# Reordering a start-up stretch: an MLP unit ahead of attention's states, two weight pieces moved forward, one filler product less

## The chip, the cores and the metric

The kernel runs on one core of a Trainium2 chip. The metric is the device time of one execution in microseconds (us). A run here means: the kernel is profiled once, its output is compared with the reference, and it is timed in several rounds that alternate with the kernel before on the same chip. Every execution reports its span and the mean clock that was granted to TensorE (1.000 is full speed). All ratios below are computed as the mean time of one kernel's fast executions over the mean time of the other's in the same rounds, with a 95% interval, so they are not quite the ratio of the medians that are quoted beside them.

Line numbers (L426 and so on) are lines of the kernel that was profiled. The change inserts lines, so one statement has two numbers; these are used below:

| statement | before | after |
|---|---|---|
| first-layer products of a unit, `plain_unit` | L426 | L435 |
| second-layer products, `plain_out` | L405 | L409 |
| activation's last step on VectorE, `plain_relu` | L442 | L453 |
| filler products "idle" | L842 | L853 |
| transposes of a part's k and q | L695 | L706 |
| scores, states | L714, L734 | L725, L745 |
| values: own chunk, then earlier chunks | L762, L773 | L773, L784 |
| running sums of the states on VectorE | L746 | L757 |
| transposes of the third part's k and q | L789 | L800 |
| weight piece: three steps on VectorE, one on GpSimd | L307, L310, L312; L314 | L310, L313, L315; L318 |
| scaling of q, k, v on GpSimd | L675 | L686 |

## The reference

Attention without a softmax, with a decay per head, and then an MLP with a PReLU, all in float32 (the constants are filled in here):

```python
# q, k, v: (8, 8, 576, 64)
scores = 64 ** -0.5 * q @ k.T                  # per batch and head
ret    = scores * where(i >= j, gamma[h] ** (i - j), 0)
attn   = ret @ v
x      = attn, heads side by side              # (4608, 512)
h      = x @ w_in                              # w_in (512, 2048)
g      = maximum(h, 0) + alpha * minimum(h, 0)
out    = g @ w_out                             # w_out (2048, 512)
```

## The kernel before

Nearly all of the time is TensorE's MLP. The change touches only the start: the first sequence's attention is computed in three "parts" (256, 256 and 64 positions), the weights are brought in as "pieces" that ScalarE, VectorE and GpSimd convert, and the first MLP "units" are put between them as soon as their inputs exist. The program issues instructions in the order of these calls, and in the traces an instruction stands behind the one ahead of it on its engine (the prediction below shows a wait of 1.99 us on VectorE that held up the piece behind it):

```python
    piece_out(2)
    part_carry(0)
    part_values(0)
    for _ in range(2):                     # filler: keeps TensorE at work
        nc.tensor.matmul(idle, ident, ...)
    nc.tensor.transpose(aps, a16, ...)
    ...
    plain_unit(0, 0)                       # the first unit
    plain_relu()
    piece_out(1)                           # the fifth piece
    part_scale(1, 2)                       # scaling of v, second part
    part_transposes(1, 0)
    piece_in(1)
    mlp_out(lambda: part_transposes(1, 1))
    piece_out(1)                           # the sixth piece
    piece_in(1)
    part_scores(1)
    piece_out(1)                           # the seventh piece
    part_states(1)                         # TensorE products, then four sums on VectorE
    piece_in(1)
    plain_unit(0, 1)                       # the second unit
    piece_out(1)                           # the eighth piece
    part_scale(2, 1)                       # scaling of q, third part
    plain_relu()
    piece_in(1)
    part_values(1)
    part_scale(2, 2)
    part_carry(1)
    last_transposes()                      # the third part's k and q
    mlp_out()                              # output products of the second unit
```

`piece_in` issues ScalarE's step of a weight piece, `piece_out` the three steps on VectorE and the one on GpSimd. `plain_unit` issues 8 products (16 records in the trace) and ScalarE's two activations; `plain_relu` issues VectorE's step after them.

Of the kernel before, what the change touches and what calls it, by code (L numbers as in the profile page):

```python
# [10 lines left out]
FP32 = mybir.dt.float32  # L11
INT32 = mybir.dt.int32
UINT32 = mybir.dt.uint32
ACTF = mybir.ActivationFunctionType
ALU = mybir.AluOpType
# [3 lines left out]
def kernel(  # L19
# [10 lines left out]
    nc = tc.nc  # L30
# [3 lines left out]
    P = 128  # L34
# [6 lines left out]
    NCC = DM // P  # L41
    NFC = DFF // P
    NU = NFC // 2
    HM = DM // 2
# [24 lines left out]
    def half(x):  # L69
        return slice(x * C, (x + 1) * C)  # L70
# [70 lines left out]
    def room(i, s0, n):  # L141
        return w_out[i][:, s0:s0 + n].rearrange("p s f -> p (s f)")
# [50 lines left out]
    for i in range(NBIT - 1):  # L193
        nc.vector.scalar_tensor_tensor(out=dif[:, i + 1], in0=dif[:, i], scalar=2.0,
                                       in1=dif[:, i], op0=ALU.add, op1=ALU.mult)
# [6 lines left out]
                            op=ALU.mult)  # L202
    nc.vector.tensor_scalar(pf, pf, 1.0, None, ALU.add)

    for o, x, y in ((slice(0, 2), slice(0, 2), slice(3, 5)), (0, 0, 1), (0, 0, 2), (1, 0, 5)):
# [7 lines left out]
                                   in1=pf[:, 6], op0=ALU.mult, op1=ALU.mult)  # L213
# [17 lines left out]
    for h2 in range(2):  # L231
# [6 lines left out]
                                       in1=tabx[hd, :, 0], op0=ALU.add, op1=ALU.mult)  # L238
# [13 lines left out]
    HI_MAX = float(np.array([0x47EFFFFF], np.uint32).view(np.float32)[0])  # L252
    HI_MIN = float(np.array([0x38000000], np.uint32).view(np.float32)[0])
# [31 lines left out]
    def piece_in(n):  # L285
        for _ in range(n):
            if npiece[1] == len(pieces):
                return
            at = npiece[1]
            npiece[1] += 1  # L290
            fetch(at + 1)
            raw, t = raws.pop(0)
            raw = raw.rearrange("p (x f two) -> p x f two", x=2, two=2)
            lo, hi = raw[:, :, :, 0], raw[:, :, :, 1]
            a = wraw.tile([P, 2, HM], FP32, tag="wa", name=f"wa_{at}")
            nc.scalar.activation(a, hi.bitcast(FP32), ACTF.Abs)

            nc.scalar.activation(lo, lo.bitcast(UINT32), ACTF.Copy, scale=2.0 ** -29)
            half_done.append((at, a, lo, hi, t))

    def piece_out(n):
        for _ in range(min(n, len(half_done))):
            at, a, lo, hi, t = half_done.pop(0)
            dst = pieces[at][1]

            c = ps_h.tile([P, 2, HM], INT32, tag="psh1", name=f"wc_{at}")
            nc.vector.tensor_scalar(c.bitcast(FP32), a, HI_MIN, HI_MAX, ALU.max, ALU.min)  # L307


            nc.vector.tensor_scalar(c, c, 3, 0x3FFFFFF8,  # L310
                                    ALU.logical_shift_left, ALU.bitwise_and)
            nc.vector.scalar_tensor_tensor(out=dst.bitcast(INT32), in0=hi, scalar=-0x40000000,  # L312
                                           in1=c, op0=ALU.bitwise_and, op1=ALU.bitwise_or)  # L313
            nc.gpsimd.tensor_tensor(out=dst.bitcast(INT32), in0=dst.bitcast(INT32), in1=lo,  # L314
                                    op=ALU.add)  # L315
            free.append(t)
            fetch(at + 1 + AHEAD)

# [100 lines left out]
    def plain_unit(kb, i):  # L419

        ph = (ps_a.tile([P, 2, TB], FP32, tag="psa", name=f"ph_{kb}_{i}") if (kb, i) == (1, 1)
              else ps_h.tile([P, 2, TB], FP32, tag="psh0", name=f"ph_{kb}_{i}"))
        g = mlp.tile([P, 8, P], FP32, tag="g", name=f"g_{kb}_{i}")
        for cc in range(NCC):
            for x in range(2):
                nc.tensor.matmul(ph[:, x], w_in[i // UST][:, cc // 2 * 2 + x, i % UST, cc % 2],  # L426
                                 xb[kb][:, cc], start=(cc == 0 and x == 0),
                                 stop=(cc == NCC - 1), skip_group_check=True)

        nc.scalar.activation(g[:, 4:8].rearrange("p x t -> p (x t)"),  # L430
                             ph.rearrange("p x t -> p (x t)"), ACTF.Relu, scale=-1.0)
        nc.scalar.activation(ph.rearrange("p x t -> p (x t)"),
                             ph.rearrange("p x t -> p (x t)"), ACTF.Relu)
        relus.append((kb, i, g, ph))

    relus = []
# [1 line left out]
    def plain_relu():  # L438
        kb, i, g, ph = relus.pop(0)
        for x in range(2):  # L440
            fc = x * NU + i
            nc.vector.scalar_tensor_tensor(  # L442
                out=g[:, 2 * x:2 * x + 2].rearrange("p m t -> p (m t)"),
                in0=g[:, 4 + 2 * x:6 + 2 * x].rearrange("p m t -> p (m t)"),
                scalar=nalpha[:, fc:fc + 1], in1=ph[:, x], op0=ALU.mult, op1=ALU.add)
        pend.append((kb, i, g))
# [98 lines left out]
    def chunk(j):  # L545
        return slice(j * C, (j + 1) * C)
# [122 lines left out]
    def part_scale(x, i):  # L669

        j0, j1 = PARTS[x]
        t = part[x][i]
        for m in range((j1 - j0 + 1) // 2):
            rows = min(P, (j1 - j0) * C)
            nc.gpsimd.tensor_tensor(  # L675
                out=t[0:rows, m], in0=t[0:rows, m],
                in1=tp[0:rows, i - 1, m, :, None].to_broadcast([rows, H, D]), op=ALU.mult)
# [26 lines left out]
    def part_scores(x):  # L704
        at = tat[x] = (mlp.tile([P, 8 * P], FP32, tag="g", name=f"pa_{x}") if x == 0 else
                       room(4, 0, 4)).rearrange("p (h n) -> p h n", h=2)  # L706
        banks = part_banks(x, 2 if x == 0 else None, "ps")
        kT, qT = tT[x, 0], tT[x, 1]
        for m in range(2):
            for c in range(NPAIR):  # L710
                for p2 in range(2):
                    for h2 in range(2):
                        j = chunk(2 * m + p2)
                        nc.tensor.matmul(banks[h2][half(p2), (2 * c + m) * C:(2 * c + m + 1) * C],  # L714
                                         kT[half(h2), c, j], qT[half(h2), c, j],
                                         start=True, stop=True)
        for h2 in range(2):
            to, fro = [t.rearrange("p (n s) -> p n s", s=C) for t in (at[:, h2], banks[h2])]
            m = mask[:, None, :].to_broadcast([P, 8, C])
            if x == 0:  # L720
                nc.vector.tensor_tensor(out=to, in0=fro, in1=m, op=ALU.mult)
            else:
                nc.scalar.copy(to, fro)
                nc.gpsimd.tensor_tensor(out=to, in0=to, in1=m, op=ALU.mult)

    def part_states(x):
        kn, vn = part[x][0], part[x][2]
        banks = [t.rearrange("p (m c d) -> p m c d", m=2, c=NPAIR)
                 for t in part_banks(x, None if x == 0 else 0, "pu")]
        for m in range(2):  # L730
            for c in range(NPAIR):
                for p2 in range(2):
                    for h2 in range(2):
                        nc.tensor.matmul(banks[p2][half(h2), m, c], kn[half(p2), m, 2 * c + h2],  # L734
                                         vn[half(p2), m, 2 * c + h2],
                                         start=(m == 0 and c == 0),
                                         stop=(m == 1 and c == NPAIR - 1), skip_group_check=True)
        was = carry[x]
        for j in range(4):
            u = banks[j % 2][:, j // 2]  # L740
            if x == 0:
                nc.scalar.copy(sums[x][j], u)
                if j:
                    nc.gpsimd.tensor_tensor(out=sums[x][j], in0=was, in1=sums[x][j], op=ALU.add)
            else:  # L745
                nc.vector.tensor_tensor(out=sums[x][j], in0=was, in1=u, op=ALU.add)  # L746
            was = sums[x][j]
# [90 lines left out]
    part_values(0)  # L838

    idle = ps_h.tile([P, DM], FP32, tag="psh0", name="idle")  # L840
    for _ in range(2):
        nc.tensor.matmul(idle, ident, part[0][0][:, 0].rearrange("p h d -> p (h d)"),  # L842
                         start=True, stop=True)
    aps = ps_a.tile([P, NFC], FP32, tag="psa", name="aps")
# [5 lines left out]
    piece_out(1)  # L850
    part_scale(1, 1)
    plain_unit(0, 0)
    plain_relu()  # L853
    piece_out(1)
    part_scale(1, 2)
    part_transposes(1, 0)
    piece_in(1)
    mlp_out(lambda: part_transposes(1, 1))
    piece_out(1)
    piece_in(1)  # L860
    part_scores(1)
    piece_out(1)
    part_states(1)
    piece_in(1)
    plain_unit(0, 1)
    piece_out(1)
    part_scale(2, 1)
    plain_relu()
    piece_in(1)
    part_values(1)  # L870
    part_scale(2, 2)
# [6 lines left out]
    piece_in(2)  # L878
    piece_out(2)
    plain_unit(1, 0)  # L880
    plain_relu()
    piece_in(1)
# [99 lines left out]
    n = 2 * NPAIR  # L982
    for b in range(2, B):
# [3 lines left out]
        at = [u + (u % NU == 0) for u in (c * nq // NPAIR + 2 for c in range(NPAIR))]  # L987
        if b == 2:
            at = [0, 3] + at[1:]
# [42 lines left out]
```

## Time and profile before

| | kernel before |
|---|---|
| time | 1011.77 us median of 3 (1010.21 to 1013.02); with three executions more, beside the changed kernel, 1011.2 |
| span of the profiled execution | 1008.5 us |
| TensorE busy | 99% |
| mean granted clock, profiled execution | 0.999 |

First the page of the kernel before: the granted clock and the share of the DMA engines in 40 slices of the span (in tenths), and the DMA queues (packets, MB, share of 16 engines).

```profile
PEclk9999999999999999999999999999999999999999
DMA  9986744232322222031122222323222000000000
...
q8 instruction: 74, 1.21, 0.5%
```

In the first 50 us, two slices, the DMA engines are busy 90% or more (a share of 0.97 from 0 to 50 us). Queue q8 carries instructions, in 74 packets of 16 KB. The kernel has 9389 TensorE products and as many weight loads; 18,778 / 74 is 254 instructions a packet. By this count, an estimate, q8 is TensorE's own queue, and a packet holds some 127 product records with their weight loads. (The page has a second queue of instructions, q14, with 33 packets and 0.27 MB: too few to be TensorE's by the same count.)

Then TensorE's timeline of the kernel before. The columns of a timeline are start, length, engine, line, operation and shape, the number of records, and in brackets the idle time before it and what ended it.

```profile
14.71 0.42 PE L773 MATMUL pv<-pT,w_out 64*32 64x64 f32 x14
16.35 1.21 PE L773 MATMUL pv<-pT,w_out 64*32 64x64 f32 x82 [1.22 <-issue]
...
36.34 1.16 PE L762 MATMUL pv<-w_out,w_out 64*64 64x64 f32 x64
37.43 1.91 PE L773 MATMUL pv<-w_out,w_out 64*32 64x64 f32 x128
```

### The profile page before, as it was taken

Reading aid. Unit: us, or ns where it says so; the run is one execution under the profiler, and the core shown is the slowest. Engines: PE = TensorE matmul, PEld = TensorE weight load, DVE = VectorE, ACT = ScalarE, POOL = GpSimd, SP = SyncE. Lnnn points to the kernel's source line nnn. Section 1 sums busy time; section 2 is a strip of 40 time slices with the busy share of each in tenths; the row PEclk is TensorE's granted clock in tenths of the full one; section 3 lists DMA queues with packets and bytes.
Section 4 is the critical chain, followed back from the end, with each engine's and each line's share of the span. In section 5 each row is a group of like instructions: output and inputs, shape, how many; then the busy total and the mean of one; then the engine's idle time right before and its main releaser. Section 6 shows DMA issues by size and latency. Waiting matters only on the chain.

```text
span 1008.5 us, 23133 instructions
## 1 busy us (share of the span) xinstructions
PE 995.2 (99%) x9389; PEld 891.9 (88%) x9389; DVE 773.4 (77%) x2086; ACT 267.3 (27%) x605; POOL 179.0 (18%) x201
## 2 busy tenths in 40 slices
PE   6999999999999999999999999999999999999998
PEld 5666668999999999999999999999999999999997
DVE  7769968887878778687777788878788776666665
ACT  5656652322222222022022121222222210000000
POOL 5656674210200020100020000200010001010000
PEclk9999999999999999999999999999999999999999
DMA  9986744232322222031122222323222000000000
GB/s 236 252 194 150 182 74 109 49 72 48 69 48 65 53 42 63 13 69 31 40 48 51 40 52 44 70 48 69 48 43 52 13 22 1 22 1 22 1 22 22
DMA packets 229595, 64.30 MB, mean 64 GB/s; under 512 B 214368, under 2 KB 223088, under 8 KB 229488
## 3 DMA queue, kind: packets, MB, share of 16 engines
q1 hardware_dynamic: 227088, 62.02, 27.4%
q8 instruction: 74, 1.21, 0.5%
q10 hardware_dynamic: 2400, 0.79, 0.4%
q14 instruction: 33, 0.27, 0.1%
HBM read 53.35 MB, written 9.44 MB: 62 GB/s over the span
## 4 chain that ended last, share of the span: by engine, by line
PE 98%; DMA 1%; issue 0%; DVE 0%; ACT 0%; SPq 0%; DVEq 0%
PE ph L470 40%; PE po L388 38%; PE ph L426 6%; PE po L405 6%; PE pv L652 3%; PE ps L616 1%; PE ps L622 1%; DMA w_out<-in_k_dram 1%; PE pv L966 1%; PE pt L695 0%; PE ps L714 0%; PE pv L773 0%; PE ps L559 0%; PE pu L734 0%; PE pu L577 0%
## 5 line engine op out<-in xcount | busy, mean ns | idle before, releaser
L388 PE MATMUL po<-w_out,g 128*128 128x256 f32 x1792 | 408.1, 379 | 0.0
L388 PEld LDWEIGHTS po<-w_out,g 128*128 128x128 f32 x1792 | 330.7, 190 | 39.7
L481 DVE TENSOR_TENSOR g<-ph,g 128x256 f32<-128x256 f32 (+1 forms) x512 | 187.0, 386 | 134.0 <-PE ph L470 67.7
L470 PE MATMUL ph<-xb,w_in 128*128 128x128 f32 x2048 | 272.7, 276 | 0.0
L470 PEld LDWEIGHTS ph<-xb,w_in 128*128 128x128 f32 x2048 | 257.1, 192 | 7.4 <-issue 0.5
L470 PE MATMUL ph<-xt,w_in 128*128 128x128 f32 x1536 | 213.3, 275 | 0.0
L470 PEld LDWEIGHTS ph<-xt,w_in 128*128 128x128 f32 x1536 | 192.1, 192 | 0.0
L476 ACT COPY g<-ph 128x128 f32<-128x128 f32 x128 | 34.1, 266 | 404.4 <-PE ph L470 391.9
L492 DVE TENSOR_TENSOR g<-g 128x128 f32<-128x128 f32 x512 | 129.4, 293 | 7.0
L531 POOL TENSOR_TENSOR qx<-qx,tabx 128x576 f32<-128x576 f32 x28 | 32.7, 1168 | 353.2 <-DMA qx<-in_q_dram 180.1
L486 DVE SCALAR_TENSOR_TENSOR g<-g 128x512 f32<-128x512 f32 x128 | 89.8, 701 | 3.0
L484 DVE TENSOR_SCALAR g<-g,alpha 128x256 f32<-128x256 f32 x256 | 85.8, 377 | 3.7
L405 PE MATMUL po<-w_out,g 128*128 128x512 f32 x128 | 58.6, 599 | 0.8 <-DVE g L442 0.8
L426 PE MATMUL ph<-xb,w_in 128*128 128x256 f32 x256 | 58.6, 383 | 0.0
L663 ACT COPY xb<-pv 128x256 f32<-128x256 f32 (+3 forms) x84 | 23.2, 315 | 126.5 <-PE pv L652 126.5
L426 PEld LDWEIGHTS ph<-xb,w_in 128*128 128x128 f32 x256 | 47.9, 190 | 9.3 <-issue 2.4
L600 ACT COPY vn<-su 64x512 f32<-64x512 f32 x56 | 34.5, 616 | 78.3 <-DVE su L594 77.9
L636 DVE SCALAR_TENSOR_TENSOR mt<-ps,th,mask 64x256 f32<-64x256 f32 x96 | 46.4, 483 | 2.2
L456 POOL TENSOR_TENSOR xt<-xb 128x256 f32<-128x256 f32 x16 | 11.6, 727 | 196.9 <-PE ph L470 196.9
L405 PEld LDWEIGHTS po<-w_out,g 128*128 128x128 f32 x128 | 23.4, 190 | 24.4 <-issue 22.8
L629 DVE SCALAR_TENSOR_TENSOR mt<-pv,th,mask 64x64 f32<-64x64 f32 x48 | 13.6, 283 | 40.2 <-ACT xb L663 39.8
L536 ACT ACTIVATE vn<-vn,tabv 64x576 f32<-64x576 f32 x56 | 43.2, 772 | 1.8 <-DMA vn<-in_v_dram 0.5
(136 smaller groups left out, 737.9 us busy)
## 6 DMA issues: line engine op xcount, KB each, us to landing
out_dram<-osb SPq DMA_DIRECT2D x34, 256.0 KB, 2.1
kx<-in_k_dram SPq DMA_DIRECT2D x112, 72.0 KB, 2.5
qx<-in_q_dram SPq DMA_DIRECT2D x112, 72.0 KB, 2.9
vn<-in_v_dram SPq DMA_DIRECT2D x56, 144.0 KB, 3.3
kn<-in_k_dram SPq DMA_DIRECT2D x56, 144.0 KB, 3.8
raw<-in_moe_w_in_dram SPq DMA_DIRECT2D x24, 256.0 KB, 4.4
raw<-in_moe_w_out_dram SPq DMA_DIRECT2D x10, 512.0 KB, 4.5
w_in<-in_moe_w_out_dram SPq DMA_DIRECT2D x6, 512.0 KB, 5.6
```

The costliest lines, as they stand in the source:

```text
L388: nc.tensor.matmul(acc[kb][n // 2][:, n % 2, :], g[:, x, :], w_out[i][:, y, :], start=(i == 0 and n % 2 == 0), stop=(i == NU - 1 and (n % ...
L405: nc.tensor.matmul(acc[kb][m], g[:, 2 * x + m], w_out[i][:, 2 * x:2 * x + 2].rearrange("p x f -> p (x f)"), start=(i == 0 and x == 0), sto ...
L426: nc.tensor.matmul(ph[:, x], w_in[i // UST][:, cc // 2 * 2 + x, i % UST, cc % 2], xb[kb][:, cc], start=(cc == 0 and x == 0), stop=(cc == N ...
L470: nc.tensor.matmul(ph[m][:, o], w_in[i // UST][:, l, i % UST, cc], r[:, cc], start=(n in (0, 3) and cc == 0), stop=(n in (2, 6) and cc == ...
L476: nc.scalar.copy(g[:, 7], ph[0][:, 2])
L481: nc.vector.tensor_tensor(out=o, in0=x0, in1=x1, op=ALU.add)
L484: nc.vector.tensor_scalar(g[:, 4 + 2 * m:6 + 2 * m], g[:, 2 * m:2 * m + 2], 0.0, alpha[:, fc:fc + 1], ALU.min, ALU.mult)
L486: nc.vector.scalar_tensor_tensor(out=g[:, 0:4].rearrange("p x t -> p (x t)"), in0=g[:, 0:4].rearrange("p x t -> p (x t)"), scalar=0.0, in1 ...
L492: ins = nc.vector.tensor_tensor(out=g[:, o, :], in0=g[:, x0, :], in1=g[:, x1, :], op=op)
L536: nc.scalar.activation(vn[x, h2], vn[x, h2], ACTF.Copy, scale=tabv[x, c:c + 1])
L600: nc.scalar.copy(vn[half(h2), h2, 1:], su[half(h2)])
L636: nc.vector.scalar_tensor_tensor(out=mt[to, h2, p2:NJ - 1:2], in0=ps[p2][half(x), 0], scalar=th[to, 3, h:h + 1], in1=mask[to, None, :].to_ ...
```

## The change

Its intent: let the second unit start without waiting, ahead of the second part's states, and bring the pieces that it needs forward on VectorE and GpSimd; start the first unit earlier, by one filler product less and by doing the piece and the activations that it needs in halves (the last products of that unit are put in an order that completes one half sooner). The diff, cut to its core:

```diff
-            nc.vector.tensor_scalar(c.bitcast(FP32), a, HI_MIN, HI_MAX, ...)
-            ... (two more on VectorE, one on GpSimd, 512 elements)
+            for f in (slice(0, P), slice(P, HM)) if at == 1 else (slice(0, HM),):
+                ... (the same four, for the second piece in two halves of 256)
@@ plain_unit
+        ... (for the first unit: the last four products sorted by half)
-        nc.scalar.activation(g[:, 4:8], ph, ACTF.Relu, scale=-1.0)
-        nc.scalar.activation(ph, ph, ACTF.Relu)
+        for x in (slice(0, 1), slice(1, 2)) if alone else (slice(0, 2),):
+            ... (the same two; for the first unit in two halves)
@@ the order of the start
-    for _ in range(2):
+    for _ in range(1):
         nc.tensor.matmul(idle, ...)
...
     plain_unit(0, 0)
+    piece_out(1)
     plain_relu()
-    piece_out(1)
-    part_scale(1, 2)
     part_transposes(1, 0)
     piece_in(1)
     mlp_out(lambda: part_transposes(1, 1))
     piece_out(1)
+    part_scale(1, 2)
     piece_in(1)
     part_scores(1)
+    plain_unit(0, 1)
     piece_out(1)
+    plain_relu()
     part_states(1)
     piece_in(1)
-    plain_unit(0, 1)
     piece_out(1)
     part_scale(2, 1)
-    plain_relu()
     piece_in(1)
     part_values(1)
```

## The prediction

> **What bounds the kernel now.** I read the page first, then busy time by stretches, then the timelines of TensorE (PE), VectorE (DVE) and GpSimd (POOL) up to 60 us, and last the order of instructions per engine of both kernels.

> ```profile
> PE 995.2 (99%) x9389; PEld 891.9 (88%) x9389; DVE 773.4 (77%) x2086; ACT 267.3 (27%) x605; POOL 179.0 (18%) x201
> ```

> TensorE is busy 99% of the span of 1008.5 us. The stretches say where its idle time ends:

> ```profile
> 20.00:30.00 10.00, 9.19 (x68) 6.18 (x70) 7.31 (x14) 6.88 (x14) 7.17 (x7) 1.00 0.98 255
> 30.00:40.00 10.00, 8.90 (x330) 7.66 (x321) 8.03 (x15) 6.10 (x12) 9.47 (x9) 1.00 1.11 298
> 40.00:50.00 10.00, 10.00 (x56) 7.03 (x54) 5.67 (x11) 5.80 (x13) 2.76 (x3) 1.00 0.80 179
> ```

> The third column is PE busy. From 40 us on there is no gap left, so whatever the change does has to happen before about 44 us, and TensorE's delay or lead there passes unchanged to the end. The change touches exactly this stretch. Idle time between 20 and 40 us is 0.81 + 1.10 = 1.9 us, and two dummy products ("idle") hide up to another 2. No version of this change can reach 2% (20 us).

> TensorE, in order of time (start, length, line, operation):

> ```profile
> 17.49 1.98 PE L842 MATMUL idle<-w_out,ident 128*128 128x512 f32 x4
> 19.62 3.69 PE L426 MATMUL ph<-xb,w_in 128*128 128x256 f32 x16
> 25.09 1.95 PE L405 MATMUL po<-w_out,g 128*128 128x512 f32 x4 [0.81 <-DVE g L442]
> 29.57 1.16 PE L714 MATMUL ps<-w_out,w_out 64*64 64x64 f32 x64
> 30.55 1.11 PE L734 MATMUL pu<-w_out,w_out 64*64 64x64 f32 x62
> 32.49 0.27 PE L734 MATMUL pu<-w_out,w_out 64*64 64x64 f32 x2 [0.83 <-issue]
> 32.69 3.72 PE L426 MATMUL ph<-xb,w_in 128*128 128x256 f32 x16
> 39.61 0.71 PE L789 MATMUL pt<-ident,w_out 64*128 64x64 f32 x8 [0.27 <-ACT xb L779]
> 40.24 3.70 PE L405 MATMUL po<-w_out,g 128*128 128x512 f32 x8
> ```

> L426 is a unit of the MLP (the first at 19.62, the second at 32.69), L405 its output products, L714/L734 the scores and states of attention's second part, L789 the transposes of its third part. The 0.83 us at 32.49 is put down to "issue", but the next instruction, the second unit, needs the sixth weight piece, which GpSimd finishes at 30.77 + 1.30 = 32.07; I read the gap as that wait. It is what the change wants to remove.

> VectorE, then GpSimd, in the same form:

> ```profile
> 24.47 0.87 DVE L442 SCALAR_TENSOR_TENSOR g<-g,nalpha,ph 128x256 f32<-128x256 f32 x2 [1.99 <-ACT ph L432]
> ...
> 32.11 0.41 DVE L746 TENSOR_TENSOR w_out<-w_out,pu 128x256 f32<-128x256 f32 x1
> 32.80 1.33 DVE L746 TENSOR_TENSOR w_out<-w_out,pu 128x256 f32<-128x256 f32 x3 [0.28 <-PE pu L734]
> 34.05 0.69 DVE L307 TENSOR_SCALAR wc<-wa 128x512 f32<-128x512 f32 x1
> ...
> 37.57 0.87 DVE L442 SCALAR_TENSOR_TENSOR g<-g,nalpha,ph 128x256 f32<-128x256 f32 x2 [1.38 <-ACT ph L432]
> ```

> ```profile
> 30.77 1.30 POOL L314 TENSOR_TENSOR w_in<-w_in,raw 128x512 int32<-128x512 int32 x1
> ...
> 36.32 1.30 POOL L314 TENSOR_TENSOR w_out<-w_out,w_in 128x512 int32<-128x512 int32 x1 [0.53 <-issue]
> 37.57 2.04 POOL L675 TENSOR_TENSOR w_out<-w_out,tp 64x512 f32<-64x512 f32 x2
> ```

> L442 is the activation's last step, L746 the four running sums of the states. L307 at 34.05 begins the eighth weight piece on VectorE; GpSimd adds its low bits at 36.32 and then scales q and v of the third part (L675). The second half of the L789 transposes reads that q. So a chain runs: sums, eighth piece on VectorE, eighth piece on GpSimd, scaling of q (done 37.57 + 1.02 = 38.6), transposes at 39.61. It has about 1 us of slack.

> [...] VectorE sits idle 1.99 us ahead of L442 at 24.47 while the fifth piece, next in its order, starts only at 25.26. This decides the case: who stands behind an instruction that waits, waits with it. [...] The trace has 0.69 us for 512 elements and 0.42 us for the L746 form of 256, so two halves cost more than one whole. [...] this trace grants 1.00 throughout the stretch [...].

> **The change part by part**, times in the trace's clock:

> 1. One dummy product of two goes: 1.98 / 2 = 0.99 us. The first unit also needs its first inputs: the last copy of the first half of xb ends about 18.33 and the first piece about 16.81 + 1.27 = 18.08. So it starts near 18.75 instead of 19.62 and ends near 22.2.
> 2. The second piece by halves: six instructions of about 0.40 us pitch for three of 0.72: 2.4 against 2.2 us, and about 0.3 with dispatch. VectorE is 0.3 us later from 18.3 on; the fourth piece ends at 22.48 + 0.3 = 22.8.
> 3. The first unit's activations by halves: ScalarE can finish all four near 23.1 instead of 24.43. Of little use because of the next point.
> 4. The fifth piece now stands ahead of L442 on VectorE and takes 2.15 us (24.47 less 22.48 was idle, 2.0 us): 22.8 to 24.95. L442 starts at 24.95 instead of 24.47, and the first output products, 0.62 us after, at 25.55 instead of 25.09: **0.5 us later** in spite of the earlier unit. The lead of point 1 is lost in this wait, and k of the second part lands only about 22.6 and 23.4 (issues at 17.23 and 17.95 plus the median of 5.4 us), so the transposes ahead gain little either.
> 5. Everything up to the scores keeps that delay: scores from 30.05 to 31.05. The sixth piece is done on VectorE at 25.75 + 2.15 = 27.9, on GpSimd, now ahead of the scaling of v, at about 29.3. So the second unit has no wait: 31.05 to 34.6, 1.6 us ahead of before (32.69). The states follow, 34.6 to 35.6. To this point TensorE has gained: before, unit and states were both done at 36.3.
> 6. But on VectorE the second unit's L442 now stands ahead of the four sums, and the sums ahead of the eighth piece. The steps after the unit's start are those of before: 3.76 us to ScalarE's first activation (32.69 to 36.45), 1.12 to L442: 31.05 + 4.88 = 35.95. L442 takes 0.8, the sums 4 x 0.42 = 1.67: the eighth piece starts on VectorE at 38.4, **4.3 us later** than 34.05. VectorE is idle from about 32.2 to 35.95.
> 7. From there, with the pitches of before: VectorE done 38.4 + 2.15 = 40.55; GpSimd 40.65 to 41.95; q scaled at 42.95; some 0.3 us for the wait, 0.3 us for four transposes, and the second unit's output products start at 43.6 instead of 40.24. TensorE meanwhile ends the values near 38.8 and stands for about 4 us.

> Sum: 43.6 - 40.24 = **+3.4 us**. The step before it (values) gained 0.5, the new wait costs 3.9. From here TensorE has no gap in which to win anything back. I round to 3.2, as the first transposes (k) may absorb a little: 1011.77 + 3.2 = 1015.0.

> **The rivals.**
> A. The intended gain. TensorE loses the 0.83 us wait and most of the dummy's 0.99, and nothing new waits: about 1 to 1.8 us faster, 1010.0 to 1010.8. For it: the wait is real, and up to the states my own working has TensorE ahead. Against it: the order of VectorE and of GpSimd is fixed in the program, and the eighth piece has to pass both ahead of q's scaling. It would be true if that scaling were not needed by L789, but the order view shows a wait on GpSimd at its second half.
> B. A wash. The transposes or other stages wait for DMA anyway (DMA share 0.98 to 1.11 between 20 and 40 us), and gains and losses are both hidden: 1011 to 1013. Against it: pieces and parts up to the eighth land by the time they are needed, since the waits in this stretch are on engines.
> C. [...], 1017 to 1018.5. [...]

> **Range and chances.** I give my working some 75%, A and B together 18%, C 7%. Times of before spread by 1.4 us each way. That gives 1015.0, a range from 1010.8 to 1018.0. Faster or slower by 2% would take 20 us out of a stretch of 25, hence 0.5% and 1%.

> **What would show it.** Right: a TensorE gap of 3 to 4 us ending near 43 us, ahead of the second half of the third part's transposes, released by GpSimd's scaling; the eighth piece on VectorE near 38.4, just after the sums; VectorE idle over 3 us ahead of the second unit's L442; the second unit at about 31 us without a wait; the first output products at 25.5. Wrong: output products of the second unit at or before 40.2 us, or the eighth piece on VectorE ahead of 36 us. Then the order that I followed is not what held TensorE, and A or B is true. A granted clock below 1.00 between 40 and 50 us would mean C.

## More of the kernel before

In the first part's values there is a pause of 1.22 us in the middle of a tile, after 14 of 96 products, put down to "issue": nothing that the profile shows was waited for. And the second part's values run through, x64 and x128, without a pause.

## The result and the profile after

The changed kernel took 1016.84 us (median of 6, 1016.36 to 1018.0) beside 1011.2 us of the kernel before (6 executions, 1010.21 to 1013.02): ratio 1.0056, interval 1.0043 to 1.0068. It is 0.6% slower, clearly so and within the 2% called the same. All values of the changed kernel are above all of the kernel before.

From the page of the changed kernel, the busy time and the clock:

```profile
PE 997.9 (98%) x9387; PEld 893.0 (88%) x9387; DVE 771.8 (76%) x2089; ACT 267.3 (26%) x607; POOL 180.0 (18%) x202
...
PEclk9899999999999999999999999999999999999999
```

One slice of PEclk fell from 9 to 8. That digit was the first sign of something that the prediction gave 7%. Busy time by stretches of the changed kernel (length, then busy time and records of PE, PEld, DVE, ACT and POOL, then granted clock, DMA share, GB/s):

```profile
20.00:30.00 10.00, 8.53 (x40) 5.97 (x39) 8.98 (x15) 6.93 (x16) 5.84 (x5) 0.93 1.03 260
30.00:40.00 10.00, 9.36 (x261) 7.17 (x260) 4.25 (x10) 6.39 (x12) 7.04 (x6) 1.00 1.11 287
40.00:50.00 10.00, 7.67 (x95) 4.65 (x95) 4.38 (x7) 5.05 (x10) 5.10 (x5) 0.66 0.81 178
```

Between 40 and 50 us TensorE was busy 10.00 us before and is busy 7.67 us now, and what it did there ran at a mean clock of 0.66. TensorE's timeline of the changed kernel:

```profile
14.48 0.42 PE L784 MATMUL pv<-pT,w_out 64*32 64x64 f32 x14
17.28 1.63 PE L784 MATMUL pv<-pT,w_out 64*32 64x64 f32 x82 [2.38 <-issue]
18.84 2.07 PE L853 MATMUL idle<-w_out,ident 128*128 128x512 f32 x2
...
21.06 3.82 PE L435 MATMUL ph<-xb,w_in 128*128 128x256 f32 x16
...
27.23 1.96 PE L409 MATMUL po<-w_out,g 128*128 128x512 f32 x4 [1.47 <-DVE g L453]
...
31.70 1.16 PE L725 MATMUL ps<-w_out,w_out 64*64 64x64 f32 x64
32.80 3.72 PE L435 MATMUL ph<-xb,w_in 128*128 128x256 f32 x16
36.45 1.16 PE L745 MATMUL pu<-w_out,w_out 64*64 64x64 f32 x64
37.43 1.11 PE L773 MATMUL pv<-w_out,w_out 64*64 64x64 f32 x64
38.47 0.89 PE L784 MATMUL pv<-w_out,w_out 64*32 64x64 f32 x48
41.76 1.81 PE L784 MATMUL pv<-w_out,w_out 64*32 64x64 f32 x80 [2.40 <-issue]
43.60 0.69 PE L800 MATMUL pt<-ident,w_out 64*128 64x64 f32 x4
44.83 0.69 PE L800 MATMUL pt<-ident,w_out 64*128 64x64 f32 x4 [0.54 <-POOL w_out L686]
45.45 5.25 PE L409 MATMUL po<-w_out,g 128*128 128x512 f32 x8
50.63 0.68 PE L809 MATMUL ps<-w_out 64*64 64x64 f32 x16
```

Three things are new. The second part's values have a pause of 2.40 us after x48, in the middle of a tile and without a releaser. The wait for GpSimd's scaling of q, which the prediction put at about 4 us, shows only 0.54. And the eight output products at 45.45 take 5.25 us where they took 3.70: the clock records have TensorE at half rate (a granted clock of 0.50) from 17.89 to 21.30 and from 41.78 to 48.61 us.

VectorE and GpSimd of the changed kernel, in the same form:

```profile
37.67 0.87 DVE L453 SCALAR_TENSOR_TENSOR g<-g,nalpha,ph 128x256 f32<-128x256 f32 x2 [4.13 <-PE pu L745]
38.46 1.85 DVE L757 TENSOR_TENSOR w_out<-w_out,pu 128x256 f32<-128x256 f32 x4
40.23 0.69 DVE L310 TENSOR_SCALAR wc<-wa 128x512 f32<-128x512 f32 x1
```

```profile
42.50 1.28 POOL L318 TENSOR_TENSOR w_out<-w_out,w_in 128x512 int32<-128x512 int32 x1 [5.12 <-issue]
43.74 2.04 POOL L686 TENSOR_TENSOR w_out<-w_out,tp 64x512 f32<-64x512 f32 x2
```

This chain is the predicted one: VectorE idle 4.13 us, activation, sums, eighth piece at 40.23, q scaled at 43.74 + 1.02 = 44.76.

Where the time went, step by step through the two profiled executions (start times on TensorE; the spans differ by 1015.2 - 1008.5 = 6.7 us):

| stretch of TensorE (first row: start of the scores; others: length, start to start) | before | after | difference |
|---|---|---|---|
| start to the second part's scores | 29.57 | 31.70 | +2.13 |
| scores to the values (unit and states between) | 6.77 | 5.73 | -1.04 |
| values to the third part's transposes | 3.27 | 6.17 | +2.90 |
| transposes to the second unit's output products | 0.63 | 1.85 | +1.22 |
| the eight output products | 3.64 | 5.18 | +1.54 |
| sum | | | +6.75 |

The sum of the rows is the whole difference of the spans: nothing is won or lost after 51 us. The intended gain is in the second row. The loss that belongs to the change is in the three rows below it. The first row is mostly the first pause (2.38 us against 1.22) and the half rate after it, with 0.7 us of step 4 below; an experiment below shows that the kernel before has it at that length too, so about 1 us of the 6.7 is chance between two profiled executions, and the timed 5.6 us is the figure to go by.

### The profile page after: what moved, and what is told of

Same layout as the page of the kernel before. It is cut to its first block, busy times and chain, and to the rows that moved or that the text cites.

```text
span 1015.2 us, 23135 instructions
## 1 busy us (share of the span) xinstructions
PE 997.9 (98%) x9387; PEld 893.0 (88%) x9387; DVE 771.8 (76%) x2089; ACT 267.3 (26%) x607; POOL 180.0 (18%) x202
## 4 chain that ended last, share of the span: by engine, by line
PE 97%; DVE 1%; DMA 1%; issue 0%; POOL 0%; ACTq 0%; DVEq 0%; POOLq 0%
PE ph L481 40%; PE po L392 38%; PE po L409 6%; PE ph L435 5%; PE pv L663 3%; PE ps L627 1%; PE ps L633 1%; DMA w_out<-in_q_dram 1%; PE pv L977 1%; PE ps L570 0%; DVE wc L313 0%; PE ps L725 0%; DVE wc L310 0%; PE pu L588 0%; PE idle L853 0%
## 5 line engine op out<-in xcount | busy, mean ns | idle before, releaser
L611 ACT COPY vn<-su 64x512 f32<-64x512 f32 x56 | 34.5, 617 | 78.6 <-DVE su L605 78.3
```

The lines of the kernel that those rows point to most:

```text
L611: nc.scalar.copy(vn[half(h2), h2, 1:], su[half(h2)])
```

## The experiments

All twelve runs gave correct results. The theory at the start was that of the prediction: the wait for the scaling of q costs the time. The rivals were the other parts of the change, and, after the first four runs, the pause marked "issue" and the clock.

### The other parts alone: undo_second_unit

The changed kernel, with the second unit back behind the states:

```diff
-    plain_unit(0, 1)
     piece_out(1)
-    plain_relu()
     part_states(1)
     piece_in(1)
+    plain_unit(0, 1)
     piece_out(1)
     part_scale(2, 1)
+    plain_relu()
```

> The changed kernel with the second unit put back behind the second part's states, all else changed. Theory O (order on VectorE: the second unit's activation and the four sums stand ahead of the eighth piece, so GpSimd scales the third part's q late and its transposes wait): nearly all of the 5.6 us goes, 1011.3 to 1012.5 us, eighth piece on VectorE back to about 34.5 us, no TensorE wait on the scaling of q. Rival F (the fifth piece ahead of the first unit's activation, the halves and the dropped dummy cost it): stays above 1014.5 us.

Measured: 1011.49 us beside 1011.7 us, ratio 0.9996 (0.9981 to 1.0011). One filler product less, the halves, and the fifth and sixth piece forward are together a wash. TensorE's timeline of this run is odd all the same:

```profile
26.46 1.96 PE L409 MATMUL po<-w_out,g 128*128 128x512 f32 x4 [1.85 <-DVE g L453]
...
40.14 1.16 PE L784 MATMUL pv<-w_out,w_out 64*32 64x64 f32 x80 [1.66 <-issue]
```

The wait on the activation is longer than the 0.81 us of the kernel before, and the pause after x48 of the values is here too, although the second unit is where it was. The granted clock was 1.00 up to 60 us (0.999 over the whole profiled execution), and the four executions had 0.998 to 1.000.

### The second unit alone: only_second_unit

The kernel before with the reverse of that edit:

```diff
+    plain_unit(0, 1)
     piece_out(1)
+    plain_relu()
     part_states(1)
     piece_in(1)
-    plain_unit(0, 1)
     piece_out(1)
     part_scale(2, 1)
-    plain_relu()
```

> The kernel before with only the second unit moved ahead of the states (its activation with it); two dummies, whole first unit, old places of the fifth and sixth piece. Theory O: most of the loss is there, 1014.5 to 1016.5 us, with the eighth piece on VectorE at about 40 us and the wait on the scaling of q. Rival F: 1011 to 1012.5 us.

Measured: 1016.78 us, ratio 1.0054 (1.0035 to 1.0072), with clocks of 0.995 and 0.996. The move of the second unit makes the whole loss. Its timeline has the pause after x47, 3.02 us long, and then half rate. No wait for the scaling of q shows in it: the transposes run as one block of eight.

```profile
41.03 1.88 PE L773 MATMUL pv<-w_out,w_out 64*32 64x64 f32 x81 [3.02 <-issue]
42.93 1.27 PE L789 MATMUL pt<-ident,w_out 64*128 64x64 f32 x8
44.12 5.15 PE L405 MATMUL po<-w_out,g 128*128 128x512 f32 x8
```

### The wait for q taken away: scale_first

```diff
     part_states(1)
+    part_scale(2, 1)
     piece_in(1)
     piece_out(1)
-    part_scale(2, 1)
     piece_in(1)
```

GpSimd scales q before the eighth piece, at 36.73 us in the trace, so nothing waits for it.

> The changed kernel with the scaling of the third part's q put ahead of the eighth piece on GpSimd; VectorE's order untouched. Theory O alone: the transposes no longer wait, the output products of the second unit start 1.2 us earlier than 45.45 if the 2.4 us gap in the values (put down to issue) and the half clock stay: about 1015.5 us. Rival I (the gap put down to issue and the half clock after it are a consequence of the order too and go with it): 1011 to 1013 us.

Measured: 1015.03 us, ratio 1.0032 (1.0013 to 1.0051). Some two of nearly six microseconds come back; more than three stay. TensorE's timeline of this run:

```profile
40.51 1.16 PE L784 MATMUL pv<-w_out,w_out 64*32 64x64 f32 x80 [1.82 <-issue]
41.94 1.00 PE L800 MATMUL pt<-ident,w_out 64*128 64x64 f32 x8 [0.28 <-ACT xb L790]
42.87 5.02 PE L409 MATMUL po<-w_out,g 128*128 128x512 f32 x8
```

The transposes run as one block of eight, so the predicted wait is gone, and the kernel is still slow. So the wait is not the only cause, and it is not needed for a loss of 3 us.

### The eighth piece early: eighth_early and eighth_early_b

Both put the eighth piece ahead of the second unit's activation on VectorE.

```diff
@@ eighth_early
     piece_out(1)
-    plain_relu()
-    part_states(1)
     piece_in(1)
     piece_out(1)
+    plain_relu()
+    part_states(1)
     part_scale(2, 1)
```

> The changed kernel with the eighth piece moved on ScalarE, VectorE and GpSimd ahead of the second unit's activation, into VectorE's idle 4.1 us. Theory O: the wait on q's scaling goes; eighth piece on VectorE at 33.6 us, q scaled before 40.5 us. With the 2.4 us issue gap and the half clock staying: about 1015.5 us; if these go too: 1010 to 1012 us.

Measured: 1016.01 us, ratio 1.0038 (1.0015 to 1.006). This edit was a mistake of mine: `plain_unit` issues ScalarE's activations itself, so the eighth piece's step on ScalarE stayed behind the unit, the piece reached VectorE only at 38.06, and the sums went back to 40.91. It is still of use for one thing: its four executions had different clocks, 1013.18 us at 1.000, 1014.82 at 0.998, 1017.62 at 0.995 and 1017.19 at 0.994. One kernel on one chip spread over 4 us, in the order of its clock but for the last pair.

The second attempt moves ScalarE's step as well:

```diff
@@ eighth_early_b
     part_scores(1)
+    piece_in(1)
     plain_unit(0, 1)
-    piece_out(1)
+    piece_out(2)
     plain_relu()
     part_states(1)
-    piece_in(1)
-    piece_out(1)
     part_scale(2, 1)
```

> As eighth_early, but with ScalarE's step of the eighth piece ahead of the second unit too, which was missed there (its activations are issued with the unit). Theory O: the eighth piece is on VectorE by 35 us, q scaled by 40 us, TensorE does not wait for it. Then only the gap put down to issue in the values is left of the new waits: 1.1 to 1.9 us better than the changed kernel, 1014.5 to 1015.8 us. If that gap was caused by the late sums or pieces, it is gone too: below 1013 us.

Measured: 1015.87 us beside 1012.09 us, ratio 1.0038 (1.0016 to 1.0061). The eighth piece is on VectorE at 35.54 us and q is scaled at 40.5 us; the wait on GpSimd is gone. What is left is the pause and the clock:

```profile
43.08 1.16 PE L784 MATMUL pv<-w_out,w_out 64*32 64x64 f32 x80 [2.82 <-issue]
...
45.55 6.41 PE L409 MATMUL po<-w_out,g 128*128 128x512 f32 x8
```

### The kernel before once more: before_again

No edit; one look, to see which pauses the kernel before has from run to run.

> The kernel before, once more, for its profile. If the first gap put down to issue (1.22 us in the values of the first part, in front of the dummies) belongs to the kernel, it is again near 1.2 us; if it varies by run, it may be 2.0 to 2.4 us as in all changed kernels so far, and then the 1.2 us of that gap is no part of the change's loss. The gap stands after 14 records of that group either way.

Measured: 1013.1 us, clock 0.998. The first pause was 2.46 us this time, not 1.22, and a half-rate stretch followed it at 18.69 to 22.10 us. In the second part there were two small pauses:

```profile
17.61 1.21 PE L773 MATMUL pv<-pT,w_out 64*32 64x64 f32 x82 [2.46 <-issue]
...
35.08 0.27 PE L734 MATMUL pu<-w_out,w_out 64*64 64x64 f32 x2 [0.51 <-issue]
...
41.00 1.21 PE L773 MATMUL pv<-w_out,w_out 64*32 64x64 f32 x82 [0.23 <-issue]
```

So the pauses belong to the kernel before as well, at fixed places: I counted TensorE's records from the start of every trace. All 26 "issue" pauses of the fourteen traces stand after record 222, 475 or 603 (once 604), whatever the tile; 603 - 475 is 128 and 475 - 222 is 253, once and twice the some 127 records of an instruction packet.

### The count of instructions shifted: page_shift and page_shift_b

The tiny transpose of `alpha` is repeated 17 and 11 times; nothing else of any size changes.

```diff
-    nc.tensor.transpose(aps, a16, ident[0:NFC, 0:NFC])
+    for _ in range(17):                    # 11 in page_shift_b
+        nc.tensor.transpose(aps, a16, ident[0:NFC, 0:NFC])
```

> The changed kernel with the small transpose of alpha done 17 times instead of once: 16 more matmul records, each with its weight load, ahead of the first unit. Theory I (the gap in the values stands at a fixed number of TensorE instructions, where the next block of instructions must be fetched): the gap moves to after 32 records of that group instead of 48. Rival (it waits for data: sums, carry): it stays at 48 or goes to a multiple of 32 that the sums set. The time may rise by up to 1 us.

> The changed kernel with ten more tiny transposes ahead of the first unit, which shifts the count of TensorE instructions by ten records and nothing else of any size. If the gap stands at a fixed count of instructions, it moves from x48 of the values to x38 exactly, a place where no tile ends and no other engine is waited for. Rival: it is a wait for another engine or a buffer, then it stays at x48 or stands at a multiple of 16. The time is expected at 1016 to 1018 either way.

Measured: 1017.41 and 1018.55 us, one execution each. With 16 records more the pause went from x48 to x32, but x32 is also where the first tile of sums is needed, and the profile named VectorE. The times speak against that label: in eighth_early the same product was let go at 41.38 us, when the first of the sums begun at 40.91 was done; in page_shift that sum was done at about 38.0 (an estimate: 37.54 and a quarter of 1.85 us), before TensorE stopped at 38.20, and x32 is again record 603. The run showed one thing besides: its pause was short (1.43 us), and now the wait for the scaling of q stood bare, 2.16 us. The shift by 10 needs no such argument. TensorE's timeline of page_shift_b:

```profile
39.29 0.77 PE L784 MATMUL pv<-w_out,w_out 64*32 64x64 f32 x38
42.13 1.32 PE L784 MATMUL pv<-w_out,w_out 64*32 64x64 f32 x90 [2.07 <-issue]
...
45.66 0.69 PE L800 MATMUL pt<-ident,w_out 64*128 64x64 f32 x4 [1.49 <-POOL w_out L686]
```

The pause moved from x48 to x38, by exactly ten records, to a place where no tile and no group of products ends. It stands at a count of instructions. And the DMA records fit. DMA in the changed kernel from 38.5 to 42 us (packets, MB, share of 16 engines):

```profile
q1 hardware_dynamic: 1046, 1.09, 94.2%
q8 instruction: 1, 0.02, 2.0%
q14 instruction: 1, 0.01, 0.6%
```

There is one packet of q8 in this time, among over a thousand packets of data that keep the engines 94% busy. It ran from 39.17 to 40.27 us; TensorE ran dry at 41.76 - 2.40 = 39.36 and went on at 41.76, 1.5 us after the packet was complete. In the kernel before the packet for the same place ran from 35.45 to 36.53 us, and TensorE came there only at 38.13. All 26 pauses, and page_shift's at x32, ended 1.2 to 1.8 us after a packet of q8 was complete. The packet of q14 in the view is not what was waited for: in undo_second_unit and only_second_unit none was complete in the 19 us before the pause ended.

### Neither pause nor wait: split_products

This is eighth_early_b with the first half of the second unit's output products (four long records) put between the states and the values:

```diff
@@ on top of eighth_early_b
-    part_values(1)
-    part_scale(2, 2)
-    part_carry(1)
-    last_transposes()
-    mlp_out()
+    mlp_out(lambda: (part_values(1), part_scale(2, 2), part_carry(1), last_transposes()))
```

> eighth_early_b with the first half of the second unit's output products put between the states and the values of the second part, so that TensorE has 1.7 us of long instructions among the 256 short ones. Theory I: the gap put down to issue shrinks by 1 us or more and the clock keeps 1.00 more often: 1011 to 1013.5 us. If the gap does not depend on what stands ahead of it, no better than eighth_early_b.

Measured: 1011.86 us beside 1012.09, ratio 1.0000 (0.9983 to 1.0017), against 1.0038 without the split. The timeline:

```profile
38.52 1.96 PE L409 MATMUL po<-w_out,g 128*128 128x512 f32 x4 [1.83 <-POOL w_out L318]
40.41 1.16 PE L773 MATMUL pv<-w_out,w_out 64*64 64x64 f32 x64
41.50 1.71 PE L784 MATMUL pv<-w_out,w_out 64*32 64x64 f32 x128
```

The values run through, x64 and x128 as in the kernel before, and the clock of the profiled stretch is 1.00. The loss is gone with the pause. The 1.83 us ahead of the products are a new wait, for GpSimd's seventh piece, and they take about what the second unit's early start had won.

### The wait for q by itself: split_late_eighth

split_products with the eighth piece late again, as in the changed kernel (the diff to the changed kernel is the `mlp_out(lambda: ...)` line above and nothing else).

> split_products with the eighth piece behind the second unit's activation and the sums, as in the changed kernel. No 256 short records stand together, so no long fetch gap and no half clock is expected at 42 us: what is left is the wait for the scaling of q alone. Theory (wait and fetch both cost, and overlap): gap on GpSimd of 1 to 2.5 us ahead of the second half of the third part's transposes, 1012.8 to 1014.5. Rival 1 (only the wait matters): 1015 or more as in the changed kernel. Rival 2 (only the fetch matters): 1011.5 to 1012.2.

Measured: 1013.25 us beside 1012.45, ratio 1.0013 (0.9993 to 1.0034). The wait on GpSimd ahead of the second four transposes was 0.92 us, there was no pause in the values, and no half rate at 42 us. That is inside the theory's 1012.8 to 1014.5, but the interval holds 1.0 too.

```profile
40.96 1.91 PE L784 MATMUL pv<-w_out,w_out 64*32 64x64 f32 x128
...
44.52 0.46 PE L800 MATMUL pt<-ident,w_out 64*128 64x64 f32 x4 [0.92 <-POOL w_out L686]
```

The size also depends on the order: here the four products, 1.95 us, lie ahead of the wait and can hide up to that much of it. What the wait costs without the pause in the changed kernel's own order was not measured.

### Is the fifth piece worth moving: split_fifth_back and undo_fifth_too

Both put the first unit's activation ahead of the fifth piece again, one on top of split_products, one on top of undo_second_unit:

```diff
     plain_unit(0, 0)
-    piece_out(1)
     plain_relu()
+    piece_out(1)
     part_transposes(1, 0)
```

> split_products with the first unit's activation ahead of the fifth piece again, as in the kernel before. If step 4 is right, the first output products wait less for VectorE (1.8 to 2.3 us in the runs with the fifth piece ahead, 0.81 in the kernel before) and start about 0.5 us earlier, and the end comes some 0.5 us earlier than split_products: 1010.5 to 1011.7, a ratio of 0.999 to 1.000. Rival: something behind the products (a weight piece or a DMA) holds the path, since the fifth piece now comes later, and nothing is gained or 0.3 us is lost.

> undo_second_unit with the fifth piece behind the first unit's activation as in the kernel before; what is left of the change is one dummy product less, the halves and the sixth piece. If step 4 is right, undo_second_unit (0.9996) gives back there what the dummy won, and this run is 0.3 to 0.7 us faster than it: 1010.7 to 1011.3, ratio 0.9990 to 0.9995. Rival: the gap is taken up by a later wait or by a fetch of instructions, and the ratio stays at 0.9996 or goes over it.

Measured: split_fifth_back 1011.49 us, ratio 0.9993 (0.9977 to 1.001), against 1.0000 for split_products. undo_fifth_too 1011.92 us, ratio 0.9994 (0.9977 to 1.0011), against 0.9996 for undo_second_unit. Both are faster by less than the intervals can tell. split_fifth_back was also the candidate to beat both kernels; it beats the changed one, and against the kernel before it is not shown to be faster. Its trace gave one more check of the count: its four products stand ahead of the values, and its pause came after x44 instead of x48.

```profile
25.39 1.96 PE L409 MATMUL po<-w_out,g 128*128 128x512 f32 x4 [1.17 <-DVE g L453]
...
41.65 1.25 PE L784 MATMUL pv<-w_out,w_out 64*32 64x64 f32 x84 [0.73 <-issue]
```

The profiled execution of undo_fifth_too, the slowest of its six with 1015.67 us, had a pause of 2.10 us after record 475 and half rate after it.

## Why the prediction was right or wrong

The time, 1016.84 us, lies in the range of 1010.8 to 1018.0 and the class is right. The size, 1.8 us over the predicted 1015.0, and the account of it are only partly right. That the time fell in the range owes something to luck: of the 3.9 us of waiting that the sum rests on, the profile shows 0.54, and a pause and a clock that the sum leaves out stand in its place.

**Steps 1 to 3, the start of the first unit.** The saving of one filler product is real. In undo_second_unit, at full clock, it is 20.05 - 17.64 = 2.41 us from the end of the first pause to the unit; before it is 19.62 - 16.35 = 3.27. That is 0.86 us, against 19.62 - 18.75 = 0.87 worked out. In the changed kernel's profile it does not show, because the first pause was 2.38 us and half rate followed: unit at 21.06 instead of 18.75. The halves of the second piece cost more than was said: 0.43 us for 256 elements against 0.69 for 512, and with the time between them the six instructions took 2.74 us (15.51 to 18.25) against 2.15 for three, 0.6 us more instead of 0.3.

**Step 4, the fifth piece ahead of the activation.** Right in direction. From the unit's start to the first output products it is 27.23 - 21.06 = 6.17 us against 25.09 - 19.62 = 5.47, 0.7 longer; in split_fifth_back, with the fifth piece back, 25.39 - 19.65 = 5.74 (in undo_fifth_too, where the transposes between waited 0.94 and 0.61 us for the DMA of k, 6.36). In the end time the two runs that undo it could not show it.

**Step 5, the second unit without a wait.** Right: unit and states are shorter by 1.04 us in the profiled pair. But the reading beneath it fell. I took the 0.83 us of "issue" as the wait for the sixth piece. It stands after record 475, where before_again, with 0.51 us, has it too: it was a fetch of instructions (in the kernel before a packet of q8 was complete at 30.67 us, 1.8 us before the gap ended at 32.49), and the label "issue" was right. The line itself speaks against the sixth piece: what follows the gap is the last two products of the states, not the unit. With the unit ahead of the states its long records come before that count, and none of the ten such traces has a pause there; of the other four three have one (0.51, 0.83 and 2.10 us).

**Steps 6 and 7, the chain over VectorE and GpSimd.** Each link has the predicted length. From the unit's start to the activation 37.67 - 32.80 = 4.87 us (4.88 worked out), from there to the eighth piece 2.56 (2.45), and from there to q scaled 44.76 - 40.23 = 4.53 (42.95 - 38.4 = 4.55). The 0.3 us that step 7 adds for the wait was an estimate; from q scaled at 44.76 to the transposes at 44.83 it was 0.07. All of it lies 1.8 us later than predicted, because the stretch ahead was late.

**The step that failed** is the one that turns this into a time: "TensorE meanwhile ends the values near 38.8 and stands for about 4 us". TensorE did not get to the end of its values. It stood in them for 2.40 us for want of instructions, then worked at half rate, and so met the wait for q with 0.54 us left. Wait and pause overlap. Without the wait but with the pause, scale_first keeps 1.0032 and eighth_early_b 1.0038, more than half of the 1.0056, and only_second_unit has 1.0054 with no wait for q in its trace. Without the pause but with 0.92 us of the wait, split_late_eighth has 1.0013, not told from 1.0. With both gone, in split_products, it is 1.0000. So most of the loss goes with the pause and the half rate behind it; what the wait costs by itself is not shown.

**Why the change brings the pause on.** In the kernel before, the second unit, 3.65 us for 16 records, stands between the states (64 records in 1.1 us) and the values (192 in 3.0 us). The change takes it out, and 256 short records stand back to back, two packets' worth. The 128 records ahead of the pause ran in some 2 us. The packet was complete 0.9 us after TensorE ran dry in the changed kernel and 1.6 us before TensorE came there in the kernel before, with the DMA engines busy while it ran in both (a share of 0.87 from 39.17 to 40.27 us, and of 1.03 from 35.45 to 36.53 before); as some 1.5 us pass from a complete packet to the next product, even the kernel before was only just in time, and in before_again it was 0.23 us late.

All fourteen traces bear this out. In seven the 128 records from 475 on are all short ones, and all seven pause at their end, by 0.78 to 3.02 us; in the other seven a unit or the split products are among them, and four have no pause, the rest 0.23, 0.73 and 1.66 us. And in all fourteen the packet for record 603 starts only after TensorE has begun record 475, 1.1 to 4.5 us after: with about 1 us for the packet and 1.4 us to the next product that is at least 3.5 us, an estimate, for a fetch that 2 us of short products are to hide. The pauses of the first 45 us, 0.23 to 3.02 us long, stand at three counts, after records 222, 475 and 603; the count between, near 349 (an estimate: 222 + 127), never showed one.

That undo_second_unit has a pause of 1.66 us at the same count shows that the move is not needed for one. There the clock stayed at 1.00 up to 60 us. What spreads the start of a packet so widely is not settled: no run varied the load on the DMA engines.

What the clock costs: six executions of the changed kernel had a mean clock of 0.9953, and 25 of the kernel before, in the rounds of the experiments, 0.9985 (8 at 1.000, 14 at 0.998, 3 at 0.997). The difference times the span is 0.0032 x 1012 = 3.2 us, an estimate, and an upper one, as TensorE did not work all of that time. Of the 5.6 us, up to 3.2 are then half rate and the other 2.4 and more TensorE standing. How these divide between fetch and wait in this order can't be told, as they overlap.

## What to carry to other kernels

When you move a long instruction out from between two runs of short ones, ask not only which engine will wait for which, but whether the instructions themselves arrive: count the records, and look for "issue" pauses at equal counts. Where TensorE bounds the kernel, the harm of a pause does not grow evenly with its length; here 1.89 us or more in one 3.41 us window cost a half-rate window as well (14 of 14), and 1.61 us or less none, so two short waits can be cheaper than one long one (2.31 us in two windows left the clock of undo_second_unit at 1.00). A label in the profile that says "waited for nothing that is shown" should be believed until a wait is proved, a releaser that it names should be checked against the time at which that was done (page_shift), and one look at the same kernel a second time tells which pauses are its own.
